# A gated-linear-attention and gated-convolution kernel on one core: pairs of PSUM banks made neighbours, a token's wait narrowed, and the order of all work replaced

## The chip, the core and the metric

The kernel runs on one core of a Trainium2 chip. The metric is the device time of one execution in microseconds (us). The core has TensorE (PE; its weight loads are listed apart as PEld), VectorE (DVE), ScalarE (ACT), GpSimd (POOL) and SyncE (SP), whose queue issues all transfers of this kernel. Each engine runs its own instructions in the order in which they were written and waits on semaphores for the others. PSUM, which PE writes and DVE and ACT read, has 8 banks of 512 float32 per partition.

## What is computed

Four sequences of 768 steps, eight heads of 48: a state decays by a gate per step and takes in k times v; q reads it. The result, as a matrix of 384 columns, goes through a gated layer.

```
f = sigmoid(f_logit)
for t in range(768):
    state = f[t][:, None] * state + outer(k[t], v[t])        # per batch and head, 48 x 48
    x[t] = q[t] @ state
gate = sigmoid(sum over j < 5 of conv_w[j] * x shifted by 4-j steps)
out  = (gate * (x @ w_val)) @ w_out
```

## The kernel before

The sequence is cut into 6 chunks of 128 steps (c = 0 to 5). In a chunk the gates are turned to logarithms, summed along the chunk, and put into q and k, so that the recurrence becomes matrix products: scores of q with k, a triangular mask, scores times v, q times the state carried over, and a new state. The gated layer is done per block of 4 x 128 rows (n = 0 to 4), and the last chunk as two halves (n = 5, 6). Its products are split into a high and a low part (three matmuls for one).

The order of all work is one text, `PROGRAM`: some 660 pieces such as `scores 4 3` or `mout 2 1`, which `run` calls one after the other; each piece writes its instructions on its engines' queues, and the class `Ordered` ties each engine to exactly that order. A piece does not wait for the pieces ahead of it in the text, only for its own data, for its buffers, and for its engine. All instructions are recorded on line 110, the helper of `Ordered`, so the profile tells them apart by their tiles:

- loads on SP: `loadf` (tile e, the gates), `loadk` (kb), `loadq` (qb), `loadv` (vb), `wload` (raw weights)
- ACT: `pexp`, `pln`, `exp2`, `exp1` (all e<-e), `kevac` (ksb<-psum), `xevac` (xf<-psum), `mhigh` (rg<-gt), `mlast`, `gate` (gt), `mstore` (osb or, in the last halves, kb <-psum)
- DVE: `scan` (e<-keep,e), `pmulk`, `pmulq` (kb, qb), `mask` (asb<-psum,tri: it reads the two banks of one scores), `mconv` (gt<-xf,cws,gt), `mlow` (xL), `mmul` (gt<-psum,gt), `mrest` (rg<-gt,rg), `stadd` (u or st)
- PE: `ktrans` (ident,kb), `scores` (qb,kb), `apply` (asb,vb and from chunk 1 qb,st), `dstate` (vb,ksb), `pconv` (xf,diag), `mval` (xH,xL with wv), `mout` (rg with wo; re in the last half)
- POOL: `stmul` (st), `halo` (xf), `turn` (mark), parts of the weights

Names of tiles carry buffer numbers in the order rows (asb_87 is the fourth mask's output, of batch 3; asb_84 that of batch 0). `scores c b` and `mask c b` go by chunk and batch; `apply c h n` by chunk, half of the batches and pass (0 or 1); `mval n m` and `mout n m` by block and third of the columns.

PSUM is one tile P of 8 banks. `Banks` deals them out while the program is written: `take` gives a piece the bank or banks that have been free for longest, `give` returns them behind the piece that reads them. `scores` and `apply` take two banks; `couple` is their view, from the lower bank to the higher with the distance between them as its step:

```
    def couple(*key):
        i, j = sorted(banks.of(key))
        return P[:, i : j + 1 : j - i]
```

Working the list by hand gives, for instance, banks 7 and 3 to `scores 4 3`, bank 5 to `mout 2 1`, banks 6 and 3 to `scores 2 1` and 4 and 1 to `scores 2 0`. What waits for what in a tile is found by the framework from the places that an instruction reads and writes.

The two passes of `apply` write the same banks, and between them stands `turn`: a small memset on POOL that waits for PE, and that the first matmul of pass 1 waits for. A second, general path for gates outside the range lies behind a branch at the end; it does not run with these inputs.

Of the kernel before, what the change touches and what calls it, by code (L numbers as in the profile page):

```python
# [38 lines left out]
weight 1; dstate 0 0; dstate 0 1; exp2 1 0; exp1 1 0; loadf 1 1; mask 0 3; weight 0; mask 0 1; scores 0 0; mask 0 0;
kevac 0 2; weight 1; pexp 2 0; pmulk 1 0; apply 0 1 0; ktrans 0 3; stadd 0 0; kevac 0 3; apply 0 0 0; weight 2;  # L40
turn 0 0; weight 0; weight 2; weight 1; dstate 0 2; dstate 0 3; loadq 1 0; ktrans 1 1; pmulq 1 0; loadk 1 1; pexp 1 1;
loadv 1 0; loadv 1 1; ktrans 1 0; kevac 1 0; pln 1 1; turn 0 1; weight 1; kevac 1 1; weight 1; apply 0 0 1; loadq 1 1;
weight 1; scores 1 0; apply 0 1 1; stadd 0 1; loadk 2 0; weight 1; weight 0; xevac 0 0; xevac 0 1; pln 2 0;
dstate 1 0; weight 2; scores 1 1; scan 1 1; weight 1; weight 2; weight 2; weight 2; msplit 0; exp2 1 1; loadf 2 1;
weight 2; exp1 1 1; mask 1 0; pconv 0; mask 1 1; weight 3; weight 3; pmulk 1 1; pmulq 1 1; weight 3; apply 1 0 0;
ktrans 1 3; gate 0 2; turn 1 0; weight 2; dstate 1 1; weight 3; weight 3; weight 3; scores 1 3; gate 0 0; weight 2;
okc 1; ktrans 1 2; apply 1 0 1; wload 2; weight 4; okc 0; loadf 3 1; kevac 1 3; weight 3; weight 3; stadd 1 0; mlow 0;
loadv 2 0; scores 1 2; gate 0 1; mval 0 0; weight 4; mask 1 3; weight 2; pexp 2 1; weight 3; mask 1 2; weight 5;
kevac 1 2; weight 4; apply 1 1 0; weight 3; stmul 1 0; weight 1; weight 1; turn 1 1; loadv 2 1; loadq 2 0; dstate 1 2;
weight 4; weight 5; mval 0 2; dstate 1 3; pln 2 1; scan 2 0; weight 4; weight 4; loadf 4 0; exp2 2 0; scan 2 1;  # L50
weight 4; halo 1; exp1 2 0; pmulk 2 0; weight 4; apply 1 1 1; loadv 3 0; loadq 2 1; mval 0 1; pexp 3 1; xevac 1 0;
stadd 1 1; xevac 1 1; weight 6; weight 6; msplit 1; mmul 0 0; mmul 0 2; weight 6; ktrans 2 0; weight 5; mmul 0 1;
ktrans 2 1; wturn 0; pexp 4 0; loadf 3 0; exp2 2 1; weight 5; kevac 2 0; stmul 1 1; loadf 4 1; kevac 2 1; loadk 2 1;
exp1 2 1; mhigh 0 2; pln 3 1; weight 6; mhigh 0 1; weight 5; weight 6; pmulq 2 0; loadq 3 0; mlow 1; weight 6;
pconv 1; scores 2 1; weight 6; mhigh 0 0; mask 2 1; pexp 3 0; loadk 3 0; weight 6; pln 3 0; loadq 3 1; scores 2 0;
dstate 2 0; weight 5; pmulk 2 1; pexp 4 1; mask 2 0; halo 2; dstate 2 1; weight 5; mrest 0 0; weight 5; pln 4 1;
mval 1 2; ktrans 2 2; stadd 2 0; apply 2 0 0; mrest 0 2; gate 1 0; mrest 0 1; kevac 2 2; mval 1 0; loadv 3 1;
scan 3 0; scan 3 1; loadk 3 1; turn 2 0; mmul 1 0; apply 2 0 1; mval 1 1; pmulq 2 1; dstate 2 2; gate 1 2; gate 1 1;
pln 4 0; xevac 2 0; mout 0 1; exp2 3 0; scan 4 1; scores 2 3; scores 2 2; mstore 0 1; pmulk 3 0; mmul 1 2; mask 2 3;
mask 2 2; exp2 3 1; mmul 1 1; exp1 3 0; loadv 4 0; loadq 4 0; pmulq 3 0; mout 0 0; scan 4 0; ktrans 2 3; ktrans 3 0;  # L60
apply 2 1 0; mout 0 2; pmulk 3 1; ktrans 3 1; mstore 0 0; send 0 0; kevac 2 3; exp1 3 1; turn 2 1; stmul 2 0;
scores 3 0; mhigh 1 0; mstore 0 2; apply 2 1 1; kevac 3 0; scores 3 1; mrest 1 0; mask 3 0; pmulq 3 1; send 0 2;
mhigh 1 1; dstate 2 3; xevac 2 1; mhigh 1 2; mask 3 1; ktrans 3 3; msplit 2; stadd 2 1; mlast 2 0; scores 3 2;
scores 3 3; kevac 3 1; okc 2; mrest 1 2; mrest 1 1; mlast 2 1; loadf 5 0; wturn 5; mconv 2 0 0; wturn 2; mask 3 3;
apply 3 0 0; turn 3 0; mconv 2 1 0; exp2 4 0; mout 1 0; mask 3 2; dstate 3 0; mlast 2 2; send 0 1; loadq 4 1;
stmul 2 1; mout 1 1; ktrans 3 2; mconv 2 0 1; exp1 4 0; wturn 4; pexp 5 0; exp2 4 1; mconv 2 1 1; wturn 1;
mconv 2 2 0; mlow 2; mconv 2 1 2; mconv 2 0 2; dstate 3 1; mconv 2 1 3; kevac 3 2; apply 3 0 1; loadk 4 0; mstore 1 1;
mconv 2 2 1; apply 3 1 0; loadf 5 1; pmulq 4 0; mstore 1 0; exp1 4 1; mval 2 2; mconv 2 0 3; loadk 4 1; mconv 2 2 2;
kevac 3 3; gate 2 1; dstate 3 2; send 1 0; turn 3 1; mconv 2 2 3; mval 2 0; stadd 3 0; pmulk 4 0; gate 2 0; loadv 4 1;
gate 2 2; pln 5 0; xevac 3 0; stmul 3 0; pexp 5 1; mmul 2 2; apply 3 1 1; mout 1 2; scores 4 1; okc 3; pln 5 1;  # L70
pmulq 4 1; wturn 3; pmulk 4 1; mmul 2 0; mhigh 2 2; mval 2 1; scan 5 0; mstore 1 2; xevac 3 1; mhigh 2 0; mask 4 1;
mrest 2 2; mmul 2 1; scores 4 0; scores 4 2; halo 3; scores 4 3; loadk 5 0; loadq 5 1; dstate 3 3; mask 4 0; mask 4 2;
exp2 5 0; ktrans 4 0; mhigh 2 1; mrest 2 0; msplit 3; ktrans 4 1; kevac 4 0; ktrans 4 2; apply 4 0 0; stadd 3 1;
mrest 2 1; dstate 4 0; loadk 5 1; kevac 4 1; mlast 3 1; turn 4 0; scan 5 1; mlast 3 0; send 1 2; mlow 3; mconv 3 0 0;
loadq 5 0; dstate 4 1; exp1 5 0; kevac 4 2; mconv 3 0 1; mask 4 3; mout 2 1; exp2 5 1; mconv 3 0 2; apply 4 0 1;
mconv 3 0 3; mconv 3 1 0; mout 2 0; stmul 3 1; ktrans 4 3; mlast 3 2; mconv 3 1 1; kevac 4 3; pmulk 5 0; exp1 5 1;
send 1 1; pmulk 5 1; mstore 2 1; apply 4 1 0; loadv 5 0; mval 3 1; gate 3 0; send 2 1; mstore 2 0; mconv 3 1 2;
dstate 4 2; mconv 3 1 3; dstate 4 3; mconv 3 2 0; mconv 3 2 1; pmulq 5 0; xevac 4 0; stadd 4 0; turn 4 1; pmulq 5 1;
apply 4 1 1; send 2 0; xevac 4 1; stmul 4 0; halo 4; mconv 3 2 2; mout 2 2; gate 3 1; mmul 3 1; mstore 2 2; mval 3 0;
scores 5 0; scores 5 3; mmul 3 0; mconv 3 2 3; mhigh 3 1; mhigh 3 0; mask 5 0; scores 5 1; mask 5 1; gate 3 2;  # L80
mval 3 2; mask 5 3; apply 5 0 0; mmul 3 2; mhigh 3 2; mrest 3 1; scores 5 2; mrest 3 0; turn 5 0; loadv 5 1; msplit 4;
mrest 3 2; mlast 4 1; stadd 4 1; mlast 4 0; mask 5 2; apply 5 0 1; mlow 4; mlast 4 2; mout 3 0; halo 5; xevac 5 0;
mconv 4 2 0; mconv 4 0 0; okc 5; mconv 4 1 0; mlast 5 1; stmul 4 1; mconv 4 0 1; mlast 5 2; mout 3 1; mconv 5 1 0;
mstore 3 0; msplit 5; apply 5 1 0; hint 3; turn 5 1; mval 4 1; mconv 4 2 1; okc 4; mconv 4 1 1; send 2 2; mconv 5 1 1;
mconv 5 2 0; mconv 4 0 2; mlast 5 0; mconv 4 2 2; mval 4 0; mconv 4 2 3; apply 5 1 1; mlow 5; xevac 5 1; mconv 5 1 2;
mconv 5 1 3; mconv 5 0 0; mconv 4 1 2; mlast 6 0; gate 4 2; mval 4 2; mconv 5 2 1; mconv 4 1 3; mout 3 2; mconv 4 0 3;
send 3 0; mval 5 1; mconv 5 2 2; mconv 5 2 3; msplit 6; gate 4 0; mstore 3 1; mmul 4 2; mconv 5 0 1; gate 5 1;
gate 4 1; mval 5 2; mconv 5 0 2; mlow 6; gate 5 2; mhigh 4 2; mmul 4 1; mmul 4 0; mval 5 0; mlast 6 1; mhigh 4 1;
mval 6 1; mconv 5 0 3; mhigh 4 0; mrest 4 1; gate 5 0; send 3 1; mlast 6 2; mrest 4 0; mval 6 2; mrest 4 2;
mconv 6 1 0; mmul 5 0; mmul 5 1; mhigh 5 0; mval 6 0; mconv 6 1 1; mconv 6 0 0; mstore 3 2; mout 4 0; mout 4 1;  # L90
mout 4 2; mconv 6 1 2; mstore 4 0; mrest 5 0; mhigh 5 1; mconv 6 2 0; send 4 0; mconv 6 2 1; mconv 6 0 1; mconv 6 1 3;
mmul 5 2; send 3 2; mrest 5 1; mconv 6 2 2; mconv 6 2 3; gate 6 1; mhigh 5 2; mrest 5 2; mout 5 0; mmul 6 1;
mconv 6 0 2; gate 6 2; mout 5 1; mhigh 6 1; mconv 6 0 3; gate 6 0; mstore 5 0; send 5 0; mout 5 2; mmul 6 2;
# [715 lines left out]
```

## Time and profile before

| | before |
|---|---|
| runs | 222.93, 223.31, 223.92 us, median 223.31 us |
| profiled execution, its own time | 224.42 us |
| its span, first to last instruction | 222.6 us |
| mean granted clock of TensorE | 0.953 |
| busy in the span | PE 177.0 us (80%), DVE 168.7 us (76%), ACT 130.3 us (59%), POOL 32.7 us (15%) |

The span is what the profile's views divide up. The profiled execution is 1.1 us above the median of the runs, and 1.8 us of its own time lie outside the span.

### The profile page before, as it was taken

Reading aid. Unit: us, or ns where it says so; the run is one execution under the profiler, and the core shown is the slowest. Engines: PE = TensorE matmul, PEld = TensorE weight load, DVE = VectorE, ACT = ScalarE, POOL = GpSimd, SP = SyncE. Lnnn points to the kernel's source line nnn. Section 1 sums busy time; section 2 is a strip of 40 time slices with the busy share of each in tenths; the row PEclk is TensorE's granted clock in tenths of the full one; section 3 lists DMA queues with packets and bytes.
Section 4 is the critical chain, followed back from the end, with each engine's and each line's share of the span. In section 5 each row is a group of like instructions: output and inputs, shape, how many; then the busy total and the mean of one; then the engine's idle time right before and its main releaser. Section 6 shows DMA issues by size and latency. Waiting matters only on the chain.

```text
span 222.6 us, 8753 instructions
## 1 busy us (share of the span) xinstructions
PE 177.0 (80%) x3964; PEld 143.3 (64%) x3964; DVE 168.7 (76%) x240; ACT 130.3 (59%) x206; POOL 32.7 (15%) x60
## 2 busy tenths in 40 slices
...
GB/s 170 358 417 426 390 17 150 257 6 177 186 276 334 265 3 180 62 167 50 67 152 213 205 202 26 241 214 1 93 90 4 3 132 50 3 47 0 97 212 37
DMA packets 11916, 33.29 MB, mean 150 GB/s; under 512 B 1504, under 2 KB 3296, under 8 KB 11616
## 3 DMA queue, kind: packets, MB, share of 16 engines
...
q8 instruction: 33, 0.54, 1.0%
...
## 4 chain that ended last, share of the span: by engine, by line
PE 61%; DVE 21%; DMA 5%; issue 5%; ACT 3%; SPq 0%; POOL 0%; DVEq 0%; ACTq 0%
PE psum L110 61%; DVE asb L110 5%; DVE gt L110 5%; DMA e<-in_f 3%; DVE xL L110 3%; DMA vb<-in_v 2%; DVE e L110 2%; DVE qb L110 2%; ACT xf L110 1%; DVE rg L110 1%; DVE cb L110 1%; ACT e L110 1%; DVE kb L110 1%; DVE ca L110 1%; DVE u L110 1%
## 5 line engine op out<-in xcount | busy, mean ns | idle before, releaser
L110 ACT ACTIVATE e<-e 128x1024 f32<-128x1024 f32 (+2 forms) x58 | 53.3, 930 | 8.9 <-DMA e<-in_f 5.5
L110 PE MATMUL psum<-rg,woH 128*128 128x512 f32 (+1 forms) x108 | 34.0, 399 | 5.3 <-DVE asb L110 5.3
L110 DVE TENSOR_TENSOR asb<-psum,tri 128x768 f32<-128x768 f32 x24 | 22.5, 953 | 19.6 <-PE psum L110 13.7
L110 PE MATMUL psum<-asb,vb 64*32 64x128 f32 (+1 forms) x1536 | 27.1, 251 | 6.7 <-issue 6.5
L110 PEld LDWEIGHTS psum<-asb,vb 64*32 64x32 f32 x1536 | 24.1, 107 | 8.7 <-issue 7.8
L110 DVE TENSOR_TENSOR_SCAN e<-keep,e 128x1024 f32<-128x1024 bf16 (+1 forms) x13 | 27.4, 2116 | 3.0 <-ACT e L110 3.0
L110 PE MATMUL psum<-qb,kb 64*64 64x128 f32 (+1 forms) x768 | 24.4, 278 | 4.9 <-DVE asb L110 4.1
L110 PEld LDWEIGHTS psum<-qb,kb 64*64 64x64 f32 x768 | 21.5, 155 | 9.5 <-DVE asb L110 5.2
L110 DVE SCALAR_TENSOR_TENSOR gt<-xf,cws,gt 128x512 f32<-128x512 f32 x36 | 25.8, 745 | 0.2
L110 PEld LDWEIGHTS psum<-rg,woH 128*128 128x128 f32 x108 | 19.7, 196 | 9.5 <-DVE asb L110 5.4
L110 ACT COPY ksb<-psum 128x384 f32<-128x384 f32 x20 | 9.4, 476 | 27.8 <-PE psum L110 23.5
L110 PE MATMUL psum<-ident,kb 128*128 128x128 f32 x80 | 13.8, 309 | 13.8 <-DVE kb L110 13.3
L110 ACT COPY xf<-psum 128x768 f32<-128x768 f32 x12 | 9.6, 797 | 23.0 <-PE psum L110 20.4
L110 PE MATMUL psum<-rg,woL 128*128 128x512 f32 (+1 forms) x54 | 21.0, 389 | 0.0
L110 PE MATMUL psum<-xH,wvH 128*128 128x512 f32 x45 | 19.8, 439 | 1.2 <-DVE asb L110 1.2
L110 PEld LDWEIGHTS psum<-ident,kb 128*128 128x128 f32 x80 | 10.0, 154 | 15.7 <-issue 13.0
L110 DVE TENSOR_TENSOR kb<-kb,e 128x512 f32<-128x512 f32 (+1 forms) x26 | 16.6, 685 | 4.4 <-DMA kb<-in_k 2.4
L110 POOL MEMSET mark<- 1x8 f32 x12 | 1.1, 95 | 121.8 <-PE psum L110 121.8
L110 DVE TENSOR_TENSOR gt<-psum,gt 128x512 f32<-128x512 f32 x15 | 10.1, 684 | 11.0 <-ACT gt L110 5.2
L110 PE MATMUL psum<-qb,st 64*32 64x128 f32 x640 | 14.7, 282 | 4.6 <-DVE asb L110 3.3
L110 PE MATMUL psum<-xL,wvH 128*128 128x512 f32 x45 | 18.2, 405 | 0.0
L110 PE MATMUL psum<-xH,wvL 128*128 128x512 f32 x45 | 18.2, 404 | 0.0
...
## 6 DMA issues: line engine op xcount, KB each, us to landing
...
```

The lines of the kernel that those rows point to most:

```text
L110: ins = emit(*a, **kw)
```

## The change

1. `Banks.take` gives two banks only as neighbours (the pair whose later freed bank has been free for longest), and a single bank by the same age with a penalty of 3 places for a bank that has a free neighbour. So `couple` always has step 1.
2. `turn` waits for the last matmul of pass 0 of its own `apply`, where it waited for the last PE instruction written so far, whatever that was.
3. `PROGRAM` holds the same 666 pieces in another order, on all engines and on SP's queue.
4. The general path is written as loops rather than unrolled; it stays behind its branch.

```
     def take(self, key, n):
-        self.held[key] = [self.free.pop(0) for _ in range(n)]
+        f = self.free
+        if n == 2:
+            pairs = [(b, b + 1) for b in f if b + 1 in f]
+            pick = min(pairs, key=lambda p: max(map(f.index, p))) if pairs else f[:2]
+        else:
+            pick = [min(f, key=lambda b: f.index(b) + 3 * (b - 1 in f or b + 1 in f))]
+        for b in pick:
+            f.remove(b)
+        self.held[key] = sorted(pick)
         return self.held[key]
...
-            if (c, h) in fence:
+            if n == 1 and (c, h) in fence:
                 after(ins, fence.pop((c, h)))
+        if n == 0:
+            fence[c, h] = ins
 
     def turn(c, h):
 
         ins = POOL.memset(mark, 0.0)
-        after(ins, PE.last)
+        after(ins, fence[c, h])
         fence[c, h] = ins
...
-loadf 0 1; pexp 0 1; pln 0 1; loadf 0 2; loadv 0 1; loadv 0 0; loadf 0 0; loadq 0 1; pexp 0 2; scan 0 1; pln 0 2;
+loadf 0 1; loadf 0 0; loadf 0 2; loadk 0 1; pexp 0 1; pln 0 1; pexp 0 2; scan 0 1; pln 0 2; loadk 0 2; pexp 0 0;
...
-mhigh 6 2; mmul 6 0; mrest 6 1; hint 1; mrest 6 2; mhigh 6 0; mstore 4 2; hint 2; mstore 5 1; mrest 6 0; mstore 4 1;
-mout 6 0; send 4 1; send 5 1; mstore 6 0; mout 6 2; mstore 5 2; rcheck; send 4 2; send 6 0; mout 6 1; hint 4;
...
+mstore 4 1; mout 4 2; mhigh 6 0; mrest 6 0; mout 5 0; mrest 6 1; mstore 4 2; mout 6 1; mout 6 2; mout 6 0; hint 2;
+mstore 6 1; send 4 1; mout 5 1; mstore 5 0; mstore 6 2; mout 5 2; send 6 2; mstore 6 0; send 6 1; send 5 0;
```

Three places of the new order. The first is SP's queue at the start of the program: the transfers it issues, f as e, k as kb, q as qb, v as vb, where 128x512 is the quarter of a chunk that is worked first. Before:

```order
1 L110 DMA e_70<-in_f 128x512
2 L110 DMA e_70<-in_f 128x1024
3 L110 DMA vb_68<-in_v 128x448 x2
4 L110 DMA e_70<-in_f 128x512
5 L110 DMA qb_64<-in_q 128x512 x2
6 L110 DMA kb_66<-in_k 128x1024
7 L110 DMA kb_66<-in_k 128x512 x2
8 L110 DMA e_71<-in_f 128x1024
```

Of the change:

```order
1 L110 DMA e_70<-in_f 128x512 x2
2 L110 DMA e_70<-in_f 128x1024
3 L110 DMA kb_66<-in_k 128x512
4 L110 DMA kb_66<-in_k 128x1024
5 L110 DMA e_71<-in_f 128x1024
6 L110 DMA qb_64<-in_q 128x512
```

The first part of k was the tenth transfer and is the fourth; v, which had the third and fourth place, now comes behind.

The second place is DVE in chunk 4, around the masks of its batches 2 and 3 (asb_86, asb_87). Before:

```order
117 L110 TENSOR_TENSOR asb_84<-psum,tri 128x768
118 L110 TENSOR_TENSOR asb_86<-psum,tri 128x768
119 L110 TENSOR_TENSOR rg_967<-gt,rg_966 128x512
120 L110 TENSOR_TENSOR u_91<-st,psum 128x384
121 L110 TENSOR_TENSOR rg_967<-gt,rg_966 128x512
122 L110 SCALAR_TENSOR_TENSOR e_72<-keep,e_72 128x1024
123 L110 TENSOR_TENSOR xL<-xf_93,xH 128x1536
124 L110 SCALAR_TENSOR_TENSOR gt<-xf_93,cws,gt 128x512 x2
125 L110 TENSOR_TENSOR asb_87<-psum,tri 128x768
```

Of the change:

```order
116 L110 TENSOR_TENSOR asb_86<-psum,tri 128x768
117 L110 TENSOR_SCALAR okc<-e_70 128x16
118 L110 SCALAR_TENSOR_TENSOR gt<-xf_93,cws,gt 128x512 x6
119 L110 SCALAR_TENSOR_TENSOR e_72<-keep,e_72 128x1024
120 L110 TENSOR_TENSOR asb_87<-psum,tri 128x768
```

The mask of batch 3 still stands behind a long piece of other DVE work: a scan, the low part xL and two convolution steps before, six convolution steps and a scan now.

The third place is DVE in chunk 0, from its first scan to its four masks. Before:

```order
6 L110 SCALAR_TENSOR_TENSOR e_70<-keep,e_70 128x512
7 L110 SCALAR_TENSOR_TENSOR e_70<-keep,e_70 128x1024
8 L110 SCALAR_TENSOR_TENSOR e_70<-keep,e_70 128x512
9 L110 TENSOR_TENSOR kb_66<-kb_66,e_73 128x2x128 x2
10 L110 TENSOR_TENSOR qb_64<-qb_64,e_70 128x512
11 L110 TENSOR_TENSOR kb_66<-kb_66,e_73 128x4x128 x2
12 L110 TENSOR_TENSOR kb_66<-kb_66,e_73 128x2x128 x2
13 L110 TENSOR_TENSOR qb_64<-qb_64,e_70 128x1024
14 L110 SCALAR_TENSOR_TENSOR e_71<-keep,e_71 128x1024
15 L110 SCALAR_TENSOR_TENSOR ca_102<-cb_103,ca_102 128x15
16 L110 TENSOR_TENSOR qb_64<-qb_64,e_70 128x512
```

Of the change:

```order
6 L110 SCALAR_TENSOR_TENSOR e_70<-keep,e_70 128x512
7 L110 SCALAR_TENSOR_TENSOR e_70<-keep,e_70 128x1024
8 L110 TENSOR_TENSOR kb_66<-kb_66,e_73 128x2x128 x2
9 L110 TENSOR_TENSOR qb_64<-qb_64,e_70 128x512
10 L110 SCALAR_TENSOR_TENSOR e_70<-keep,e_70 128x512
11 L110 TENSOR_TENSOR kb_66<-kb_66,e_73 128x4x128 x2
12 L110 TENSOR_TENSOR qb_64<-qb_64,e_70 128x1024
13 L110 TENSOR_TENSOR kb_66<-kb_66,e_73 128x2x128 x2
14 L110 TENSOR_TENSOR qb_64<-qb_64,e_70 128x512
15 L110 SCALAR_TENSOR_TENSOR ca_102<-cb_103,ca_102 128x15
16 L110 TENSOR_TENSOR asb_86<-psum,tri 128x768
```

The scan of chunk 1 (e_71, 128x1024) stood ahead of chunk 0's masks and now follows them, and the first quarter's k and q (rows 8 and 9) come ahead of a scan.

## Rows read from the trace of the kernel before

**Rows 1.** Busy time of the engines, from the page: us, share of the span, instructions.

```profile
PE 177.0 (80%) x3964; PEld 143.3 (64%) x3964; DVE 168.7 (76%) x240; ACT 130.3 (59%) x206; POOL 32.7 (15%) x60
```

**Rows 2.** What PE's matmuls and what DVE's masks waited for, over the span: us in total, times, the longest in us.

```profile
PE psum L110 <- DVE asb L110: 16.7, 12, 5.3
...
PE psum L110 <- issue: 6.5, 5, 2.2
PE psum L110 <- POOL mark L110: 0.8, 3, 0.3
...
DVE asb L110 <- PE psum L110: 13.7, 7, 4.3
```

**Rows 3.** PE's timeline around six of its waits for a mask: start us, us busy, what, and in brackets the idle time just before and what ended it.

```profile
73.92 0.89 PE L110 MATMUL psum<-qb,kb 64*64 64x128 f32 x30 [1.91 <-DVE asb L110]
...
103.73 0.67 PE L110 MATMUL psum<-vb,ksb 128*64 128x48 f32 x16 [1.15 <-DVE asb L110]
...
141.51 1.14 PE L110 MATMUL psum<-vb,ksb 128*64 128x48 f32 x32
147.93 1.22 PE L110 MATMUL psum<-rg,woH 128*128 128x512 f32 x2 [5.28 <-DVE asb L110]
...
171.27 0.89 PE L110 MATMUL psum<-qb,kb 64*64 64x128 f32 x30 [0.88 <-DVE asb L110]
...
173.32 0.50 PE L110 MATMUL psum<-xH,wvH 128*128 128x512 f32 x1 [1.16 <-DVE asb L110]
...
179.67 0.53 PE L110 MATMUL psum<-qb,st 64*32 64x128 f32 x20 [1.00 <-DVE asb L110]
```

**Rows 4.** DVE's timeline ahead of the wait of 5.28 us, in the same columns.

```profile
140.43 0.68 DVE L110 TENSOR_TENSOR rg<-gt,rg 128x512 fp32r<-128x512 f32 x1
141.03 2.28 DVE L110 TENSOR_TENSOR_SCAN e<-keep,e 128x1024 f32<-128x1024 bf16 x1
143.23 2.33 DVE L110 TENSOR_TENSOR xL<-xf,xH 128x1536 fp32r<-128x1536 f32 x1
145.49 1.53 DVE L110 SCALAR_TENSOR_TENSOR gt<-xf,cws,gt 128x512 f32<-128x512 f32 x2
146.93 0.95 DVE L110 TENSOR_TENSOR asb<-psum,tri 128x768 f32<-128x768 f32 x1
```

**Rows 5.** PE's and DVE's timelines around chunk 3's first mask, in the same columns.

```profile
99.44 0.90 PE L110 MATMUL psum<-qb,kb 64*64 64x128 f32 x32
...
101.69 0.90 PE L110 MATMUL psum<-qb,kb 64*64 64x128 f32 x32
...
102.72 0.96 DVE L110 TENSOR_TENSOR asb<-psum,tri 128x768 f32<-128x768 f32 x1 [2.89 <-PE psum L110]
```

**Rows 6.** Stretches of 5 us, of 30 us in the last row: bounds, length, then for PE, PEld, DVE, ACT and POOL the busy us and (instructions), the granted clock of TensorE, the share of the DMA engines, GB/s.

```profile
75.00:80.00 5.00, 5.00 (x44) 4.05 (x39) 5.00 (x9) 4.94 (x9) 1.13 (x2) 0.66 0.27 106
145.00:150.00 5.00, 2.07 (x5) 1.69 (x6) 4.92 (x7) 0.36 (x1) 0.00 (x0) 0.72 0.61 225
150.00:155.00 5.00, 5.00 (x105) 3.88 (x104) 4.94 (x8) 0.00 (x0) 0.00 (x0) 0.60 0.00 2
...
180.00:210.00 30.00, 30.00 (x415) 25.48 (x398) 28.00 (x56) 14.71 (x31) 0.10 (x1) 1.00 0.15 57
```

**Rows 7.** The start: timelines of ACT, DVE and PE, in the columns of rows 3.

```profile
5.53 1.06 ACT L110 ACTIVATE e<-e 128x1024 f32<-128x1024 f32 x1 [0.62 <-DMA e<-in_f]
...
6.72 2.09 ACT L110 ACTIVATE e<-e 128x1024 f32<-128x1024 f32 x3
...
7.80 3.41 DVE L110 TENSOR_TENSOR_SCAN e<-keep,e 128x1024 f32<-128x1024 bf16 x2 [1.63 <-ACT e L110]
12.54 0.76 DVE L110 TENSOR_TENSOR kb<-kb,e 128x256 f32<-128x256 f32 x2 [1.33 <-DMA kb<-in_k]
13.22 0.68 DVE L110 TENSOR_TENSOR qb<-qb,e 128x512 f32<-128x512 f32 x1
...
13.07 1.19 PE L110 MATMUL psum<-ident,kb 128*128 128x128 f32 x4 [13.07 <-DVE kb L110]
```

**Rows 8.** DVE's timeline at the masks of chunk 0, in the same columns.

```profile
20.00 1.82 DVE L110 TENSOR_TENSOR asb<-psum,tri 128x768 f32<-128x768 f32 x2
...
22.07 1.93 DVE L110 TENSOR_TENSOR asb<-psum,tri 128x768 f32<-128x768 f32 x2
```

**Rows 9.** The longest of PE's five waits in which the profile shows no releaser, and from the page the queue that carries instructions (packets, MB, share of 16 engines).

```profile
44.17 0.74 PE L110 MATMUL psum<-asb,vb 64*32 64x128 f32 x38 [2.22 <-issue]
...
q8 instruction: 33, 0.54, 1.0%
```

**Rows 10.** The end: the last piece of PE and the copy behind it, from the chain of work that ended last (start us, us, what).

```profile
179.67 36.32 PE psum L110 x445
...
216.01 0.37 ACT kb L110
```

**Rows 11.** Groups of instructions by form: busy us, mean ns of one, idle time before.

```profile
L110 PE MATMUL psum<-re,woH 128*128 128x256 f32 x18 | 3.2, 280 | 0.0
L110 DVE SCALAR_TENSOR_TENSOR gt<-xf,cws,gt 128x512 f32<-128x512 f32 x36 | 25.8, 745 | 0.2
L110 DVE TENSOR_TENSOR asb<-psum,tri 128x768 f32<-128x768 f32 x24 | 22.5, 953 | 19.6 <-PE psum L110 13.7 <-ACT cb L110 4.5 <-ACT xf L110 1.2
```

More of the change, by code (lines that the diff above doesn't have):

```diff
@@ L39 @@
[L39 to L93, printed above, removed]
@@ new lines @@
+weight 0; weight 1; exp2 1 0; apply 0 0 1; kevac 0 3; turn 0 1; pmulk 1 0; exp1 1 0; weight 1; loadq 1 1; loadk 1 1;
+weight 2; loadf 2 1; weight 2; apply 0 1 1; ktrans 1 0; ktrans 1 1; pmulq 1 0; stadd 0 0; weight 1; weight 1;
+dstate 0 3; xevac 0 0; scan 1 1; okc 0; weight 2; xevac 0 1; kevac 1 0; kevac 1 1; weight 2; weight 1; loadf 2 0;
+scores 1 0; mask 1 0; weight 1; pexp 2 1; scores 1 1; exp2 1 1; weight 1; pconv 0; weight 3; weight 3; wload 2;
+weight 3; exp1 1 1; mask 1 1; loadv 1 1; weight 2; weight 3; weight 3; pmulk 1 1; apply 1 0 0; okc 1; loadv 2 1;
@@ new lines @@
+loadk 2 0; dstate 1 0; dstate 1 1; msplit 0; ktrans 1 3; turn 1 0; gate 0 1; gate 0 0; ktrans 1 2; weight 2; weight 2;
+gate 0 2; kevac 1 2; weight 3; kevac 1 3; weight 2; stadd 0 1; weight 2; apply 1 0 1; weight 3; weight 3; weight 4;
+pln 2 1; weight 2; pmulq 1 1; halo 1; loadk 2 1; scores 1 3; pexp 2 0; scores 1 2; mlow 0; loadq 2 0; stadd 1 0;
+mval 0 0; mask 1 3; loadf 3 0; weight 1; dstate 1 2; pln 2 0; weight 3; mask 1 2; loadf 3 1; weight 5; scan 2 1;
+weight 3; exp2 2 1; weight 4; apply 1 1 0; scan 2 0; loadq 2 1; exp2 2 0; exp1 2 0; turn 1 1; weight 4; weight 4;
@@ new lines @@
+weight 6; pexp 4 0; pln 3 1; weight 6; kevac 2 2; apply 2 0 0; weight 6; loadk 4 0; mhigh 0 0; pln 4 0; mval 1 2;
+mrest 0 1; turn 2 0; mrest 0 2; kevac 2 3; weight 6; wturn 0; gate 1 2; apply 2 0 1; weight 5; weight 6; pmulq 2 1;
+mrest 0 0; xevac 2 0; dstate 2 2; loadf 4 1; loadq 3 0; gate 1 1; mout 0 0; scan 3 0; stmul 2 0; mstore 0 0; scan 3 1;
+loadk 3 0; gate 1 0; scan 4 0; scores 2 3; exp2 3 0; dstate 2 3; scores 2 2; wturn 4; mmul 1 2; send 0 0; exp2 3 1;
+loadq 4 0; loadf 5 0; pexp 4 1; mout 0 1; mask 2 3; halo 2; mask 2 2; pmulk 3 0; mval 1 0; pln 4 1; apply 2 1 0;
@@ new lines @@
+loadk 3 1; exp1 3 1; exp1 3 0; turn 2 1; loadv 3 1; mout 0 2; exp2 4 0; mhigh 1 2; mmul 1 0; stadd 2 1; scan 4 1;
+mstore 0 1; wturn 3; apply 2 1 1; pmulq 3 1; pmulq 3 0; pexp 5 0; pmulk 3 1; ktrans 3 0; mval 1 1; send 0 1;
+xevac 2 1; stmul 2 1; kevac 3 0; exp1 4 0; mrest 1 2; scores 3 3; scores 3 2; loadf 5 1; scores 3 1; mmul 1 1;
+mhigh 1 0; mhigh 1 1; mlast 2 2; mask 3 3; loadk 4 1; mrest 1 1; mstore 0 2; mrest 1 0; scores 3 0; mask 3 1;
+ktrans 3 1; mout 1 2; exp2 4 1; mlast 2 0; mlast 2 1; exp1 4 1; loadq 4 1; pmulq 4 0; mout 1 1; msplit 2; ktrans 3 3;
```

125 lines of the change are left out of this document (73 added, 52 removed).

## The prediction, on record before the changed kernel ran

> **What bounds the kernel now.** I read the busy times first. PE is busy for 177.0 of 222.6 us and DVE for 168.7 [rows 1], so neither is full, and two engines that feed each other share the bound. The chain that ended last says where there is no slack at all: from 179.67 us to 215.99 it is one piece of PE without a gap [rows 10]. What can be won lies before that. PE starts at 13.07 us [rows 7], and its matmuls then wait 16.7 us for masks, 6.5 us for nothing that the profile shows, and 0.8 us for the token [rows 2].
>
> Then I took the waits for masks one by one, with the banks that the list deals out, and asked for each whether the waiting matmul uses a bank or a result of that mask. Six do not [rows 3]. The clearest is `mout 2 1`. It writes bank 5, and the last product that it reads, a rest (rg), is done by 141.11 us [rows 4]. PE is free at 142.65 (141.51 + 1.14), and starts at 147.93, 0.05 us behind the end of a mask at 147.88 [rows 3, 4]. That mask is `mask 4 3`. It reads banks 7 and 3, and the view `couple` goes from 3 to 7 in steps of 4: bank 5 lies between. The wait looks like one on everything from the lowest to the highest place that the mask reads. The other five have the same form: `scores 2 0` (banks 1 and 4) is stopped in its second bank until a mask of banks 3 and 6 is through, 1.91 us; `dstate 2 3` in bank 3 by a mask of 1 and 7, 1.15; `scores 5 1` in bank 4 by a mask of 1 and 6, 0.88; `mval 3 2` in bank 2 by one of 0 and 4, 1.16; `apply 5 0 1` in bank 1 again by one of 0 and 4, 1.00 [rows 3]. Together 11.4 us of the 16.7.
>
> DVE pays the same way. `mask 3 0` reads banks 0 and 6. Its own scores end at 100.34 (99.44 + 0.90), yet it waits until 102.72, behind the scores that PE runs from 101.69 to 102.59 into banks 1 and 7 [rows 5]: some 2.3 of its 2.89 us are for a bank between. Such waits are part of DVE's 13.7 us [rows 2].
>
> **The change, part by part.**
>
> *Neighbouring banks.* With step 1 nothing lies between, so the six waits lose their cause: 11.4 us. I do not take all of it. The last three (0.88 + 1.16 + 1.00 = 3.0 us) lie close to the piece from 180 us on in which DVE too is busy for 28.0 of 30 us [rows 6]; there PE can come earlier only if DVE does, and I take half, 1.5. That leaves 9.9. Bounds: 0, if the wait has another cause, and 11.4.
>
> *The clock behind the lulls.* After the wait of 1.91 us the granted clock of 75 to 80 us is 0.66 while PE is busy throughout: 0.34 x 5 = 1.7 us lost to the lower of the two levels. After that of 5.28 us it is 0.72 and then 0.60 [rows 6]. The second stretch loses 0.40 x 5 = 2.0; the first is low for 2.8 us (0.28 x 5 x 2), of which 2.07 run with PE busy, 1.0 lost. Without the lulls this goes: 4.7 us. Bounds: 0, if other lulls come in their place, and 4.7.
>
> *The opening.* DVE's first k product waits for its transfer until 12.54 us, and PE's first transpose starts 0.53 us behind it [rows 7]. That k was the tenth transfer and is the fourth. What is late next is the second part of f, now third in the queue: ACT takes it at 5.53 us, and 256 KB ahead of it cost some 0.8 us (half of the 2 us that separates the two first takings, an estimate). Its two passes, and the scan that started at 7.80, move to about 8.6; the scan (2.28) ends at 10.9, and the first transpose comes at about 11.4, 1.6 us earlier. From there DVE has two k-and-q pairs of a quarter (0.76 + 0.68 each), a scan of 1.2, and a pair of a half (1.3 + 1.2) before its first mask [rows 7, 8]: 6.6 us, so about 17.5, and four masks to 21.2. Before, they ended at 24.0 (22.07 + 1.93) [rows 8]; the scan of chunk 1 no longer stands ahead of them. That is 2.8 us; since q now lands behind two more transfers, I take 2.5. Bounds: 0 and 2.8.
>
> *The end.* In the old list three pieces of `mout` follow the last rest of DVE, now five do. A piece of this width is a third of 3.2 us [rows 11]. With DVE as full as it is there, two more pieces behind it cost 2.1 us. Bounds: 0, if DVE is done early, and 2.1.
>
> *The long DVE piece in chunk 4.* `mask 4 3` stands behind six convolution steps and a scan: 6 x 0.745 + 2.28, and its own 0.95, is 7.7 us [rows 4, 11]. Who waits for it is `apply 4 1 0`. Ahead of that PE has two `mout` and two passes of `apply` with transposes, some 9 us by the same pieces of the old run, so I take nothing; without that cover it is up to 7.7.
>
> *The token.* PE waits for it three times, 0.8 us in all [rows 2]; the narrower wait can give back no more, and POOL's work behind it only comes earlier. I take 0, inside the rounding.
>
> *The general path* does not run. What it could change is the fetching of instructions: the queue that brings them moved 33 packets [rows 9]. I take nothing; bounds: a gain or loss of the longest unexplained wait, 2.2 us.
>
> *Waits that nothing shows.* The 6.5 us of these lie almost all in runs of small `apply` matmuls [rows 2, 9]. Those runs are as long as before, so I leave the 6.5 us as they are. The Trainium skill, Runtime: NRT & Kernel Launch, section Instruction fetch mechanics, says that code comes in blocks of 16 KiB by a queue of the engine's own, and that crossing a block is mostly hidden. The packet size agrees (0.54 MB in 33 packets); by that rule these waits would be something else, and the sum stays the same.
>
> The sum on the profiled execution's span: 222.6 - 9.9 - 4.7 - 2.5 + 2.1 = 207.6 us. The median of the runs was 0.7 us above that span (and 1.1 below that execution's own time), so 208.3, and I say 208 us.
>
> **Rivals.**
>
> *DVE takes over.* The order lets PE run, but DVE, with 168.7 us of work, keeps its own idle time: 13.7 us of waits for PE at masks, and its waits for ACT. If half of the 15 us gained comes back as true waits of PE for DVE: 222.6 - 7.5 = 215 us. For it: DVE is as full as PE after 180 us. Against: in the old run DVE waits for PE about as much as PE for its masks, so the two idle in turn, and shortening one shortens the other.
>
> *A shortage of banks, and slower.* The waits are for banks that are truly used, and the neighbour rule makes them scarcer: a pair must take two given banks, even ones just given back. The place is `scores 4 2`, which by the new list gets banks 6 and 7 directly behind the mask of `scores 4 0`. The price is a mask with its handover, about 1.1 us, less what PE does meanwhile. To pass 223.3 it needs some 14 such waits in full, of 24 scores. Against: the old run's longest wait was for a bank that no one used, and two `dstate` and a transpose stand between those two scores. 225 us. The skill's page Perfetto Trace Analysis, section Identifying Performance Opportunities, reads the same gap repeating on the engine that should be saturated as too little PSUM for the next tile; that would be this rival, and rows 3 do not bear it out, since bank 5 was free.
>
> *The steps of the views are not the cause.* Then the six waits stay in some form, and only the opening and the end change: 222.6 - 2.5 + 2.1 = 222.2, no change.
>
> *More than I take.* The remaining true waits for masks (16.7 - 11.4 = 5.3) and the token's 0.8 go as well, and the end costs nothing: 207.6 - 5.3 - 0.8 - 2.1 = 199.4 us.
>
> **How the numbers follow.** The forecast, 203 to 212 us: 0.60. DVE takes over, 212 to 219: 0.22. More, below 203: 0.07. No change: 0.05. Slower: 0.06. A measurement of this kernel tells about 0.5% from no change. The range is that of the forecast, most of DVE's rival and half of the better one: 199 to 219, with 0.05 + 0.06 and some of the tails left out. Faster by over 0.5%: 0.60 + 0.22 + 0.07 = 0.89; within: 0.05; slower: 0.06.
>
> **What would show it.** PE's waits for masks fall from 16.7 to some 6 us, and none ends with a mask of banks that the matmul does not use; DVE's waits at masks fall from 13.7 by half or more. No stretch of PE's work in the middle has a clock of 0.6 behind a lull of 5 us. The first transpose starts near 11.4 us and the fourth mask ends near 21. The last piece without a gap starts earlier than 179.67. It is wrong if PE's waits are as long and only have other names, if DVE is busy for over 90% while PE waits for it, or if the unexplained waits, 6.5 us now, grow with PE's small matmuls packed closer.

## The result, and the profile after

The changed kernel takes 197.31 us (median; 195.04 to 201.66 us), the kernel before 223.62 us in the same comparison: 0.876 of the time, 95% interval [0.868, 0.885]. That is faster, as forecast, but below the range of 199 to 219 us. The profiled execution was one at a mean granted clock of 0.977 and took 201.66 us, above its median; a second profile of the same kernel, from experiment e5, ran at 1.000 and stands beside it.

Busy times of the changed kernel and its instruction queue, from the page, to be read against [rows 1] and [rows 9]:

```profile
PE 172.6 (86%) x3964; PEld 137.7 (69%) x3964; DVE 169.8 (85%) x240; ACT 130.2 (65%) x206; POOL 33.9 (17%) x60
...
q8 instruction: 32, 0.52, 1.1%
```

What its PE and its DVE waited for (us in total, times, the longest), against [rows 2]:

```profile
PE psum L110 <- DVE kb L110: 12.4, 1, 12.4
PE psum L110 <- issue: 8.7, 8, 2.8
PE psum L110 <- DVE rg L110: 1.5, 1, 1.5
...
DVE bad L110 <- PE psum L110: 6.0, 1, 6.0
...
DVE asb L110 <- PE psum L110: 4.8, 6, 2.8
```

PE has no wait for a mask left, where it had 16.7 us, and none for the token. DVE's waits at masks fell from 13.7 to 4.8 us, and PE and DVE are now busy for 86 and 85% of the span. The same in e5's profile, first busy times, then waits, then span and mean granted clock:

```profile
PE 170.4 (87%) x3964; PEld 137.1 (70%) x3964; DVE 169.7 (87%) x240; ACT 130.5 (67%) x206; POOL 35.6 (18%) x60
```

```profile
PE psum L110 <- issue: 5.1, 7, 1.4
PE psum L110 <- ACT rg L110: 0.9, 1, 0.9
PE psum L110 <- DVE rg L110: 0.8, 1, 0.8
```

```profile
die 0 (median of its cores): 195.3 us, clock 1.000
```

Since PE's busy time, its waits and what lies behind its last matmul make up the span, the difference can be booked line by line (us; from the views above and the same views of before; some tenths are lost where instructions overlap):

| | before | changed | changed (e5) |
|---|---|---|---|
| up to the first transpose | 13.1 | 12.4 | 12.7 |
| PE busy | 177.0 | 172.6 | 170.4 |
| PE waits for masks | 16.7 | 0 | 0 |
| PE waits that nothing shows | 6.5 | 8.7 | 5.1 |
| PE's other waits | 2.9 | 1.9 | 2.6 |
| from PE's last matmul to the end of the span | 6.6 | 4.2 | 4.2 |
| span | 222.6 | 199.9 | 195.3 |

PE's last piece, from the chain that ended last in the changed kernel (start us, us, what), against [rows 10]:

```profile
160.04 35.70 PE psum L110 x401
```

The last piece without a gap starts at 160.04 us, 19.6 earlier than before, and is about as long. And the opening (start us, us busy, what, in brackets the idle time and what ended it), against [rows 7] and [rows 8]:

```profile
7.43 1.06 ACT L110 ACTIVATE e<-e 128x1024 f32<-128x1024 f32 x1 [2.17 <-DMA e<-in_f]
...
12.40 1.19 PE L110 MATMUL psum<-ident,kb 128*128 128x128 f32 x4 [12.40 <-DVE kb L110]
...
19.67 2.69 DVE L110 TENSOR_TENSOR asb<-psum,tri 128x768 f32<-128x768 f32 x3 [0.32 <-PE psum L110]
```

The first transpose comes at 12.40 us, 0.7 earlier than before, and chunk 0's masks end at 22.36 (19.67 + 2.69), 1.6 earlier than before's 24.0. In e5's profile of the same kernel they end at 23.41, 0.6 earlier.

### The profile page after: what moved, and what is told of

Read it like the earlier page. It is cut to its first block, busy times and chain, and to the rows that moved or that the text cites. A ratio compares the mean times of both kernels' runs of the same rounds, so it can differ in the third digit from the quotient of the medians.

```text
span 199.9 us, 8759 instructions
## 1 busy us (share of the span) xinstructions
PE 172.6 (86%) x3964; PEld 137.7 (69%) x3964; DVE 169.8 (85%) x240; ACT 130.2 (65%) x206; POOL 33.9 (17%) x60
## 4 chain that ended last, share of the span: by engine, by line
PE 80%; DMA 6%; issue 6%; DVE 4%; ACT 1%; SPq 1%; DVEq 0%
PE psum L110 80%; DMA vb<-in_v 3%; DMA e<-in_f 3%; DVE qb L110 2%; ACT e L110 1%; DVE kb L110 1%; DVE e L110 1%; SPq L110 1%; DVE rg L110 0%; ACT kb L110 0%; DVEq L110 0%
## 5 line engine op out<-in xcount | busy, mean ns | idle before, releaser
L110 PE MATMUL psum<-rg,woH 128*128 128x512 f32 (+1 forms) x108 | 33.3, 391 | 1.5 <-DVE rg L110 1.5
L110 PE MATMUL psum<-asb,vb 64*32 64x128 f32 (+1 forms) x1536 | 25.6, 247 | 4.1 <-issue 3.8
L110 PEld LDWEIGHTS psum<-asb,vb 64*32 64x32 f32 x1536 | 23.1, 105 | 5.6 <-issue 5.0
L110 PE MATMUL psum<-ident,kb 128*128 128x128 f32 x80 | 14.0, 303 | 13.5 <-DVE kb L110 12.4
L110 PE MATMUL psum<-qb,kb 64*64 64x64 f32 (+1 forms) x768 | 23.2, 269 | 1.4 <-issue 1.2
L110 PEld LDWEIGHTS psum<-qb,kb 64*64 64x64 f32 x768 | 20.3, 148 | 5.3 <-issue 3.4
L110 PE MATMUL psum<-xH,wvH 128*128 128x512 f32 x45 | 19.0, 422 | 0.0
L110 ACT COPY osb<-psum 128x512 f32<-128x512 f32 x15 | 8.7, 585 | 12.6 <-PE psum L110 10.7
L110 DVE TENSOR_TENSOR qb<-qb,e 128x1024 f32<-128x1024 f32 (+1 forms) x13 | 15.3, 1183 | 0.0
L110 ACT CAST rg<-gt 128x512 fp32r<-128x512 f32 x15 | 9.3, 620 | 8.6 <-DVE gt L110 6.9
```

The source lines that it names most:

```text
L110: ins = emit(*a, **kw)
```

## The experiments

My theory: the views over two distant banks make PE and DVE wait for banks between, and nearly all of the gain is that. The rival: the searched order makes the gain. They were parted by undoing each in the other's company.

**Old order, neighbouring banks.** The kernel before with the new `Banks.take`, nothing else.

```
-        self.held[key] = [self.free.pop(0) for _ in range(n)]
+        f = self.free
+        if n == 2:
+            pairs = [(b, b + 1) for b in f if b + 1 in f]
+            pick = min(pairs, key=lambda p: max(map(f.index, p))) if pairs else f[:2]
+        else:
...
```

> The old order with nothing changed but the dealing of banks: pairs are neighbours. If waits on banks that lie between the two of a view are the cause of the six waits (11.4 us) and of the low clock behind two of them, PE's waits for masks fall from 16.7 to about 5 us and the time to 207 to 213 us. If the gain of the change is that of the new order, or if the waits are for banks truly in use, it stays at 221 us or more.

Measured: 206.64 us, 0.926 [0.911, 0.941]. PE's and DVE's waits:

```profile
PE psum L110 <- issue: 7.8, 6, 2.4
PE psum L110 <- DVE asb L110: 3.2, 4, 2.0
...
DVE asb L110 <- PE psum L110: 7.1, 3, 4.4
```

Which banks are dealt out is worth 7.4% with the old order. PE busy fell to 171.4 us as well.

**New order, old dealing.** The changed kernel with the old `take`.

```
-        f = self.free
-        if n == 2:
-            pairs = [(b, b + 1) for b in f if b + 1 in f]
...
+        self.held[key] = [self.free.pop(0) for _ in range(n)]
```

> The new order and the rest of the change, but banks dealt out as before, so that views have steps over 1 again. If the step is the cause, waits of PE for masks come back (more than 8 us) and the time lies between 203 and 215 us. If the order alone makes the gain, it stays within 2% of the changed kernel, 194 to 200 us.

Measured: 227.8 us, 1.022 [1.010, 1.035]. Its waits:

```profile
PE psum L110 <- DVE asb L110: 14.4, 11, 3.9
...
PE psum L110 <- ACT xf L110: 10.5, 8, 2.3
...
DVE asb L110 <- PE psum L110: 26.9, 12, 7.0
```

The searched order with distant banks is slower than the kernel before. So the order does not make the gain by itself, and the rival falls.

**Old order, old banks, one bank per instruction.** This parts "the view spans banks" from "other banks are dealt": banks as before, but `mask` and `xevac` as two instructions, each on one bank.

```
-        aps = couple("scores", c, b)[:, :, 0:384].rearrange("k s (p t) -> k s p t", p=2)
...
+        for s, at in enumerate(sorted(banks.of(("scores", c, b)))):
+            aps = P[:, at, 0:384].rearrange("k (p t) -> k p t", p=2)
+            DVE.tensor_tensor(out=ASB[b][:, s], in0=aps,
+                              in1=tri[:].unsqueeze(1).to_broadcast([128, NP // 2, 192]), op=ALU.mult)
...
+        for s, at in enumerate(sorted(banks.of(("apply", c, h)))):
+            ACT.copy(XF[c % 2][:, :, 2 * h + s, HALO:], P[:, at, 0 : NM * C].rearrange("p (m t) -> p m t", m=NM))
```

> The old order and the old dealing, but the mask and the copy of an apply read their two banks in two instructions, one bank each, so that no view spans others. 24 more instructions on DVE and 12 on ACT. If the span of the view is the cause, the wait of mout 2 1 for the mask of batch 3 (5.28 us) goes although the banks are the same ones, and the time falls to 209 to 217 us, a little behind the neighbours since DVE pays some 0.1 us for each added instruction. If the banks themselves are scarce, the waits stay and the time is 223 us or more.

Measured: 204.29 us, 0.916 [0.906, 0.926], although DVE has 24 and ACT 12 instructions more. All of PE's waits that come to over 0.5 us in total:

```profile
PE psum L110 <- DVE kb L110: 13.2, 3, 12.6
PE psum L110 <- issue: 11.1, 6, 4.5
PE psum L110 <- POOL mark L110: 0.8, 3, 0.3
```

With the same banks, dealt to the same pieces in the same order, no wait for a mask is left. What makes PE wait is the span of the view, not the bank. The edit also halves each mask and copy; that this is not what helps is seen two experiments on, where the same halving without spans gains nothing.

**New order, old dealing, one bank per instruction.** The same edit on the kernel of the second experiment.

> The changed kernel with the old dealing of banks, but masks and copies of an apply read bank by bank, so that pairs lie apart and no view spans others. If the span alone is the cause, the new order keeps its gain without neighbours: 194 to 201 us, and no wait of PE for a mask over 2 us. If neighbours matter by themselves (as to which banks come free when), it stays at 205 us or more.

Measured: 199.94 us, 0.889 [0.880, 0.900]:

```profile
PE psum L110 <- issue: 8.5, 6, 2.2
```

No wait for a mask is left, and the longest other one is 1.7 us, for a rest (rg). The new order loses 2% with spans and gains some 3% on the old order without them (0.916 to 0.889; it also has the looped path).

**The changed kernel, one bank per instruction too.**

> The changed kernel with neighbours, masks and copies of an apply read bank by bank: nothing is left to win from spans, 36 instructions more. If spans are all that reading both banks at once costs, it is the changed kernel's time or up to 1% more. If a mask or copy of half the size lets PE or DVE start earlier, it is up to 2% less.

Measured: 200.35 us, 0.897 [0.888, 0.905], above the 0.872 [0.860, 0.885] of the changed kernel in the same comparison (e5, next), and the intervals do not overlap. With neighbours nothing is left for the edit to free, and its instructions cost.

**The changed kernel again, and with the old token.** The second lets `turn` wait for the last PE instruction written so far, and the first matmul of either pass for its token, as before the change.

```
-        after(ins, fence[c, h])
+        after(ins, PE.last)
```

> The changed kernel as it is, for its time and its profile on the chip of the following three: 195 to 199 us.

> The changed kernel, but the token waits for the last PE instruction written, as before. If the narrower wait matters only with the new order, PE waits for the token by 1 to 4 us more and the time is 1 to 2% above the changed kernel. If it is worth nothing, as predicted, the two agree within 0.5%.

Measured: 196.65 us, 0.872 [0.860, 0.885], and 197.26 us, 0.880 [0.866, 0.893]. With the old token PE waits for it again:

```profile
PE psum L110 <- POOL mark L110: 1.4, 5, 0.3
```

The narrower wait takes away 1.4 us of PE's waits; the times can't tell the two apart.

**The general path.** Old order with the looped path, and the changed kernel with the unrolled one; the path runs in neither.

Of the edit that makes the loops:

```
-        def pair(b, pp, odd):
...
-            for e in range(D):
...
-        with tc.For_i(0, B, 1) as b, tc.For_i(0, NP // 2, 1) as pp:
-            for odd in range(2):
-                pair(b, pp, odd)
...
+        with tc.For_i(0, B * NP // 2, 1) as i, tc.For_i(0, 2, 1) as odd:
...
+            with tc.For_i(0, D, 1) as r:
```

> The old order with the general path, which does not run, written as loops. The end from PE's last matmul to the end of the span was 6.5 us before and is 4.1 us after. If the length of the code that is jumped over sets it, it falls to about 4 us and the time by 2 us, to 221 us. If it is set by the last transfers or the order at the end, no change (within 0.5%).

> The changed kernel with the general path unrolled as before. If the length of the code behind the branch costs time at the end, the stretch from PE's last matmul to the end of the span grows from some 4 us to over 6 and the time by some 2 us, 1%. If it costs nothing, within 0.5% of the changed kernel.

Measured: 222.66 us, 0.996 [0.990, 1.002] for the first, 198.81 us, 0.882 [0.869, 0.894] for the second: neither time says much. The traces do. PE's last piece in the chain, of the old order with loops (span 220.5 us):

```profile
179.93 36.32 PE psum L110 x445
```

And of the changed kernel unrolled (span 202.7 us):

```profile
160.19 35.67 PE psum L110 x401
```

From the end of PE's last matmul (216.25 and 195.86) to the end of the span it is 4.25 us with loops and 6.8 without, against 6.6 before (222.6 - 215.99) and 4.2 in the changed kernel. PE's end hardly moves in either pair. Which work it is shows in the instruction queues in the last 7 us (packets, MB, share). Changed kernel, then unrolled, then the kernel of e8, whose DVE and ACT have 36 instructions more:

```profile
q8 instruction: 1, 0.02, 1.1%
q14 instruction: 3, 0.02, 1.0%
```

```profile
q8 instruction: 2, 0.03, 2.4%
q14 instruction: 5, 0.04, 1.6%
```

```profile
q14 instruction: 4, 0.03, 1.2%
q8 instruction: 1, 0.02, 0.9%
```

Four packets go with 4.2 us, seven with 6.8, and e8's five with 5.7 us (span 196.1, PE's end 190.35), so looped code alone doesn't give the short end: it goes with how many blocks of code are still fetched when the work is over. All the traces here fall into line: 4.1 to 4.4 us with four packets (eight traces), 5.7 and 6.0 with five (e8 and e7), 6.6 to 6.8 with seven (the kernel before, e1, e3, e12). The edit of the path forced four and seven in both orders; five was seen, not forced. That the fetching itself is what takes the time was not tested apart. The end also accounts for 1.5 us of what e8 loses.

**What are the waits that nothing shows?** Counting the matmuls from the start up to such a wait, in windows of the changed kernel that end there (columns as [rows 6]; the count of PE is in its bracket):

```profile
0.00:24.00 24.00, 10.37 (x221) 8.43 (x221) 17.06 (x24) 14.72 (x25) 6.33 (x21) 1.00 0.91 339
0.00:28.00 28.00, 13.55 (x349) 11.02 (x349) 19.96 (x30) 18.04 (x30) 7.11 (x24) 1.00 0.85 318
...
0.00:39.30 39.30, 21.57 (x604) 16.53 (x604) 31.16 (x46) 27.96 (x44) 10.09 (x26) 1.00 0.80 295
```

With one after 476 they stand 127 or 128 matmuls apart, and each matmul has its weight load: 256 instructions of PE. The other four of its eight waits stand after 1114, 3027, 3282 and 3537 matmuls: 4, 15, 2 and 2 such blocks on. The kernel before, whose order puts other work at these counts, has its five waits after 220, 348, 475, 730 and 2390 matmuls, two of them here:

```profile
0.00:30.20 30.20, 14.59 (x348) 12.08 (x348) 24.25 (x37) 21.13 (x36) 7.41 (x24) 1.00 0.85 327
...
0.00:44.10 44.10, 25.19 (x730) 19.39 (x731) 33.52 (x47) 30.86 (x48) 10.47 (x26) 1.00 0.74 276
```

So places at the same distance from the start of the code show waits in both orders. To test it, 32 matmuls on a tile of zeros were put at the very start, where PE is idle; the work itself is whole.

```
-loadf 0 1; loadf 0 0; loadf 0 2; loadk 0 1; pexp 0 1; pln 0 1; pexp 0 2; scan 0 1; pln 0 2; loadk 0 2; pexp 0 0;
+loadf 0 1; loadf 0 0; loadf 0 2; loadk 0 1; pexp 0 1; pln 0 1; pexp 0 2; scan 0 1; pln 0 2; loadk 0 2; pexp 0 0; busy 32;
```

> The changed kernel with 32 matmuls of zeros into a free bank ahead of PE's first transpose, in time in which PE waits anyway. In the profile of the changed kernel PE's unexplained waits stand after 221, 349, 476, 604 matmuls, 127 or 128 apart. If they come at borders of blocks of instructions that are fetched, they stand after the same counts with the 32 counted, that is 32 matmuls earlier in the work: the longest, inside the convolution's 120 matmuls after its 68th, moves to its 36th. If they belong to the work at those places (its data, its transfers), they stay where they are in the work, after counts larger by 32. The time says little here.

Measured, one execution: 198.32 us. Its windows up to the waits:

```profile
0.00:23.80 23.80, 18.86 (x221) 10.97 (x222) 15.69 (x24) 14.25 (x25) 5.80 (x21) 0.86 0.91 341
0.00:29.20 29.20, 22.38 (x349) 13.95 (x349) 20.76 (x31) 18.47 (x31) 6.50 (x24) 0.88 0.80 305
0.00:32.70 32.70, 24.58 (x477) 15.86 (x477) 24.22 (x36) 19.63 (x32) 6.50 (x24) 0.87 0.75 280
```

These waits come after the same counts, so 32 matmuls earlier in the work; they belong to the place in the code and not to the work at it. Its other two stand after 732 and 987 matmuls, again on the grid of 128. The longest one, after 604, did not move as I expected: here no wait stands after 604 matmuls or after 636. The queue agrees: 32 packets of 16 KB, and PE's 2 x 3964 instructions are 31 times 256.

**Two tries to do better.** First the second part of f back to second place in SP's queue.

```
-loadf 0 1; loadf 0 0; loadf 0 2; loadk 0 1; pexp 0 1; pln 0 1; pexp 0 2; scan 0 1; pln 0 2; loadk 0 2; pexp 0 0;
+loadf 0 1; loadf 0 2; loadk 0 1; loadf 0 0; pexp 0 1; pln 0 1; pexp 0 2; scan 0 1; pln 0 2; loadk 0 2; pexp 0 0;
```

> The changed kernel with the second half of chunk 0's gates second in SP's queue, ahead of the other quarter, and the first k third. If the start hangs on that transfer (ACT takes it at 7.43 us against 5.53 before), ACT takes it by 6.5 us, the first transpose comes at 10.9 to 11.7 instead of 12.4, and the time falls by up to 1.2 us. If what is late next is something else (the other quarter's gates, q), the first transpose comes earlier but the four masks of chunk 0 end at the same 22.4 us, and the time is unchanged within 0.5%.

Measured: 199.18 us (194.72 to 201.68), undecided against the changed kernel's 195.04 to 201.66. Its opening (columns as before):

```profile
6.28 1.06 ACT L110 ACTIVATE e<-e 128x1024 f32<-128x1024 f32 x1 [0.88 <-DMA e<-in_f]
...
11.26 1.19 PE L110 MATMUL psum<-ident,kb 128*128 128x128 f32 x4 [11.26 <-DVE kb L110]
...
27.63 1.49 PE L110 MATMUL psum<-asb,vb 64*32 64x128 f32 x99 [1.65 <-issue]
```

The start gains the 1.1 us it was to gain (12.40 to 11.26), and chunk 0's masks end 1.0 earlier too (21.35). But the wait after 349 matmuls is 1.65 us, where it was 0.83 in the changed kernel and 0.56 in e5, and nothing is left that a time could show.

Then the third transfer of weights earlier, away from the longest of these waits (2.77 us, after 604 matmuls).

```
-weight 0; weight 1; exp2 1 0; apply 0 0 1; kevac 0 3; turn 0 1; pmulk 1 0; exp1 1 0; weight 1; loadq 1 1; loadk 1 1;
+weight 0; weight 1; exp2 1 0; apply 0 0 1; kevac 0 3; turn 0 1; pmulk 1 0; exp1 1 0; weight 1; loadq 1 1; loadk 1 1; wload 2;
...
-scores 1 0; mask 1 0; weight 1; pexp 2 1; scores 1 1; exp2 1 1; weight 1; pconv 0; weight 3; weight 3; wload 2;
+scores 1 0; mask 1 0; weight 1; pexp 2 1; scores 1 1; exp2 1 1; weight 1; pconv 0; weight 3; weight 3;
```

> The changed kernel with the transfer of the output weights (1152 KB, issued at 31.6 us) put behind chunk 1's last k, some 8 us earlier in the queue. If PE's unexplained wait at 36.7 to 39.4 us (2.77 us) is long because its block of instructions is fetched beside that transfer, it falls to 1.4 us or less and others beside the moved transfer grow. If its length has nothing to do with transfers, it stays at 2 us or more. Time within 1% either way.

Measured: 198.56 us (196.27 to 201.48), undecided as well:

```profile
30.48 1.49 PE L110 MATMUL psum<-asb,vb 64*32 64x128 f32 x99 [2.75 <-issue]
```

The wait after 604 matmuls is gone, and that after 349 grew from 0.83 to 2.75 us, beside the transfer in its new place: that is what a wait would do that is long because a transfer runs alongside. One execution doesn't show it. With the transfer in its old place the wait after 604 was 2.77 and 1.39 us in two profiles of one kernel and is absent in e6 and e9; the one after 349 was 0.28 to 1.97 us in the other runs that show it.

## Why the prediction was right, and where it was wrong

**Cause and sign were right.** That matmuls wait for masks of banks they don't use, because of the view's span, is shown by e3, which keeps banks and order and removes the span; e8 shows that the halving that comes with it is worth nothing.

**The waits for masks: the step that failed.** I took off 9.9 us and left 6.8 (16.7 - 9.9); all 16.7 went. The step was "Together 11.4 us of the 16.7", with the other 5.3 as true waits, as the matmul does use the mask's bank or result. The six that I left in are these in the kernel before:

```profile
54.64 0.67 PE L110 MATMUL psum<-qb,st 64*32 64x128 f32 x32 [1.12 <-DVE asb L110]
55.50 1.05 PE L110 MATMUL psum<-asb,vb 64*32 64x128 f32 x64 [0.19 <-DVE asb L110]
...
106.29 2.84 PE L110 MATMUL psum<-qb,kb 64*64 64x128 f32 x64 [1.30 <-DVE asb L110]
110.32 0.67 PE L110 MATMUL psum<-qb,st 64*32 64x128 f32 x32 [1.19 <-DVE asb L110]
115.14 0.67 PE L110 MATMUL psum<-vb,ksb 128*64 128x48 f32 x16 [1.05 <-DVE asb L110]
...
138.64 1.53 PE L110 MATMUL psum<-ident,kb 128*128 128x128 f32 x12 [0.47 <-DVE asb L110]
```

And these are the masks just ahead of them:

```profile
53.62 1.82 DVE L110 TENSOR_TENSOR asb<-psum,tri 128x768 f32<-128x768 f32 x2 [4.31 <-PE psum L110]
...
105.28 0.96 DVE L110 TENSOR_TENSOR asb<-psum,tri 128x768 f32<-128x768 f32 x1 [0.47 <-ACT xf L110]
...
109.21 0.96 DVE L110 TENSOR_TENSOR asb<-psum,tri 128x768 f32<-128x768 f32 x1 [0.56 <-PE psum L110]
...
114.12 0.96 DVE L110 TENSOR_TENSOR asb<-psum,tri 128x768 f32<-128x768 f32 x1 [3.29 <-PE psum L110]
...
137.62 1.82 DVE L110 TENSOR_TENSOR asb<-psum,tri 128x768 f32<-128x768 f32 x2 [1.32 <-PE psum L110]
```

With the banks that the list deals out, four of the six have the very form of those that I had found; I had sorted them wrongly. Each starts 0.05 to 0.15 us behind the end of a mask whose result it doesn't read, and it writes none of that mask's two banks, only banks between them: `scores 3 2` (banks 2 and 6) behind `mask 3 1` of 1 and 7, 1.30 us; `apply 3 0 0` (3 and 7) behind `mask 3 3` of 1 and 4, 1.19; `dstate 3 0` (4) behind `mask 3 2` of 2 and 6, 1.05; `ktrans 4 0` (1) behind `mask 4 0` of 0 and 4, 0.47. That is 4.0 us, of which some 0.3 are a copy on ACT that reads bank 2 until 105.25. The other two, 1.12 and 0.19 us, are true: `apply 1 1 0` takes over banks 2 and 7 of `mask 1 3` and reads its result and that of `mask 1 2`. But both masks came late. Their scores end at 48.41 and 51.24 us; `mask 1 3` starts at 53.62, 0.10 us behind `mval 0 0`, which writes bank 6, between 2 and 7. DVE had been idle for 4.31 us by then. I wrote that "DVE pays the same way", but booked nothing for it. So ten of the twelve waits, 15.4 of 16.7 us, come straight from the span, and the other 1.3 from a mask that the span held up. With the old order and no spans (e3) all are gone. The half that I kept of the last three (1.5 us), because DVE is full there, was wrong as well.

One reading of [rows 3] was wrong without harm: the mask that holds up `dstate 2 3` at 103.73 is `mask 3 0` of 0 and 6, which ends at 103.68, not one of 1 and 7. Bank 3 lies between either way.

**The clock.** Forecast 4.7 us, measured as PE's busy time: 4.4 (177.0 to 172.6) to 6.6 (170.4, at a clock of 1.000). The size was right, but in part by luck. I booked the stretches behind two lulls; the kernel before has two more of 5 us, 45 to 50 at 0.68 and 105 to 110 at 0.66. And in the changed kernel's first profile two others are low (columns as [rows 6]), behind a wait of 2.77 us that nothing shows and one of 1.53 us for a rest:

```profile
40.00:45.00 5.00, 5.00 (x144) 2.24 (x123) 4.56 (x7) 1.99 (x4) 0.00 (x0) 0.66 0.02 6
80.00:85.00 5.00, 4.51 (x44) 3.37 (x46) 5.00 (x4) 1.60 (x3) 0.00 (x0) 0.66 0.79 225
```

In e5's profile none is low before PE's end.

**The opening.** Forecast 2.5 us at the masks, measured 1.6, and 0.6 in e5's profile. The mis-sized term is the second part of f: I let 256 KB ahead of it cost 0.8 us; ACT takes it at 7.43 instead of 5.53 us, so 1.9. With that part second again (e10) it is 6.28, so 1.15 of the 1.9 are the place in the queue. The scan and the first transpose follow it, as I had them.

**The end.** The 2.1 us for more of `mout` behind DVE's last rest did not come: DVE is done early enough to wait 6.0 us at its last instruction, and PE's last piece has no gap. My lower bound of 0 ("if DVE is done early") was the case.

**The general path.** I took 0, with 2.2 us of gain or loss as bounds; it gave 2.4 us at the end of the span, where I had not looked. I had let the code cost at the unexplained waits only; the 6.6 us behind PE's last matmul were in no term of the sum.

**The token.** PE's 0.8 us of waits for it are gone; in the time e6 can't be told from the changed kernel, so 0 was near enough. **The waits that nothing shows** stayed about as they were: 6.5 before, 8.7 and 5.1 after. I doubted that they were borders of code blocks. The Trainium skill, Runtime: NRT & Kernel Launch, section Instruction fetch mechanics, says that code comes in blocks of 16 KiB, or 256 instructions, and that crossing one is mostly hidden. Of some 31 borders four to eight show a wait in the runs here, which agrees with "mostly"; but these cost up to 4.5 us each (e3), and I was wrong to read the rule as saying that they must be something else.

**The rivals.** "DVE takes over" did not happen: DVE's busy share rose with PE's, and its waits for PE shrank. "A shortage of banks" and "the steps are not the cause" fall with e1 and e3. What happened is the one that I gave 0.07, "more than I take": remaining waits for masks and the token's gone, no cost at the end, 199.4 us of span. With the 2.4 us of the general path that is 197.0; the two profiles have 199.9 and 195.3. I had called those remaining waits true, so the rival's number came out for another reason than it gave. All twelve waits had one cause, so they came or stayed together; a range of independent halves was too cautious on that side.

**Order and banks.** I gave the order, apart from the opening and the end, nothing. With distant banks it costs 2% (1.022, e2), but on top of neighbours order, token and general path together bring 0.926 to about 0.875. So my theory's "nearly all of the gain" was too much: neighbours alone give 7.4 of some 12.5%. From e1's trace to e5's, PE loses 3.2 us of waits for masks, 2.4 at the end (the general path), 2.7 of waits that nothing shows, 1.0 of busy time and 1.6 of waits for q and the token, and gets 1.7 for rests (rg): 9.2 of the 9.0 us between the spans (204.3 and 195.3). These are single executions, and the 2.7 would be -0.9 with the other profile of the changed kernel. So what is the order's own is at most a few us, and how much of it is a search that knew the dealing stays open.
